# Copies that spread token lists move from GpSimd to DVE, and a slot loads all of the next w2 at its own end

## The chip, the cores and the metric

The kernel runs on one core of a Trainium2 chip. The metric is the device time of one execution in microseconds, as the median of several runs. The engines are named as the profile names them: PE (TensorE matmul) and PEld (its weight load), DVE (VectorE), ACT (ScalarE), POOL (GpSimd) and SP (SyncE, which here only issues transfers). A q behind an engine's name (SPq) means its instruction queue.

## The reference, cut to what matters

Attention with a sigmoid in place of the softmax is followed by a mixture of experts in which each token goes to one expert.

```python
def _attn_ref(q, k, v):                 # (8, 12, 448, 64) each
    scores = scale * q @ k.T - log(S)
    return (1 / (1 + exp(-scores))) @ v
...
def _moe_ref(x, w_gate, w_output_gate, w1, w2):   # x: (3584, 768), 8 experts
    logits = x @ w_gate
    e_idx = argmax(logits, axis=1)
    gate_w = softmax(logits)[e_idx]
    eom = sigmoid(x @ w_output_gate)
    for e in range(8):                  # w1[e]: (768, 1024), w2[e]: (1024, 768)
        mask = e_idx == e
        out[mask] = gate_w * eom[:, e] * (relu(x[mask] @ w1[e]) @ w2[e])
```

## The kernel before, in words

**Stages.** Up to about 270 us the kernel computes attention, batch after batch, writes the rows to DRAM (`x_dram`) and routes the finished batches: each token gets a place in its expert's list in DRAM (`lst`). After that it works through slots. A slot is one expert with up to 256 tokens of its list: layer 1 (x times w1, eight groups `f` of 128 hidden units), then layer 2 (h times w2, two halves of tokens by two halves of columns). PE computes in a split form: every operand is a high part, made by a cast on ACT, and a low part, made by a subtraction on DVE, so each weight that arrives is first split (`split_w1`, `split_w2`, lines 578 to 600).

**Kinds of slots.** In this execution there are eleven slots of 256 tokens (numbers 0 to 10, function `slot`), three of 192 tokens (`wide_slot`, 640 to 724 us) and two of 128 tokens (`half_slot`, from 724 us on). Slots 0 to 3 are straight code; the later ones stand in nested conditional blocks, since only the routing says how many of each kind there are. Where a block isn't entered, each engine jumps to the end of the nest and there raises the semaphores that the left-out code would have raised.

**The order of work in a slot.** The order on each engine is the order in which the program is written; nothing is reordered. In layer 1, group `f` of PE fills one of three PSUM banks (`self.psh`, cut to three at line 1048), ACT copies half of it (L631), DVE adds the other half (L632), ACT applies the ReLU (L636) and DVE makes the low part (L637). PE can't begin group f+3 before DVE's L632 of group f has read its bank. After layer 1 come, for the next slot: `turn_x` (a transposition of the gathered tokens on DVE, L605), the gather of the tokens of the slot after the next (POOL, indirect DMAs, L545, into the one buffer `xg` that `turn_x` has just read), the split of x and w1, and beside them PE's layer 2.

**Lists.** A gather needs its token numbers spread over 128 partitions, and so does the scatter of the output. `spread_lists` (L498), `spread_two` (L510) and `spread_rest` (L524) do that: DVE transposes a block of 32 partitions (L501, L513), and then POOL makes four times three small copies, one set of three for each group of 32 destination partitions, out of the same 32 source partitions. Two `spread_lists` of 12 copies stand in the attention stage (`unit`, u = -31 and -8). The rest is done from the generator `side()` (lines 1004 to 1045), which is advanced between the steps of slots 0 to 3: counting its steps, one `spread_lists` falls in slot 1 right behind `turn_x`, one `spread_two` in slot 2 behind group 2, one `spread_two` in the layer 2 of slot 2, and in slot 3 a `spread_lists` behind group 1, a `spread_lists` behind group 3 and `spread_rest` (8 small instructions) behind group 4. Slot 3 also has a POOL drain (L696) ahead of its gather.

**w2 around the 192-token slots.** w2 comes in four transfers of two rows of blocks each (rows 0, 2, 4, 6 of `w2r`). A 192-token slot uses raw w2 in `layer2_q` (L725) for 64 of its tokens, so `w2r` comes free late. It loads rows 0 and 2 of the next w2 behind `layer2_q` (L760), and at its end leaves the next expert's number and a flag in two words (`held`, DVE copy L764). The slot that follows, wide or half, begins with `load_held` (L574): SP loads two registers from those words (L539) and issues rows 4 and 6 (L566), then loads two registers for the slot after, and issues that slot's w1.

Of the kernel before, what the change touches and what calls it, by code (L numbers as in the profile page):

```python
# [42 lines left out]
LATE_F = LATE_MAX + 2  # L43
LATE_N = LATE_F + E + 2
GT = 32
LGR = LATE_N // 4
# [8 lines left out]
def r32(ap):  # L55
    return ap.bitcast(F32)


class Kernel:
# [80 lines left out]
    def constants(self):  # L140
        nc = self.nc
# [64 lines left out]
        own = gl[1].bitcast(I32)  # L206
        a = TS
# [10 lines left out]
        self.ltb = own[:, a:a + 2 * E].rearrange("p (k h w) -> p k h w", h=1, w=2)  # L218
        a += 2 * E
        self.at = own[0:GT, a:a + LGR + 1]  # L220
        a += LGR + 1
        self.held = own[0:1, a:a + 2]

    def row_words(self):
        v, tok = self.nc.vector, self.tok
# [181 lines left out]
    def table_late(self):  # L407
        v = self.nc.vector
# [9 lines left out]
        first = self.tmp_off  # L418
# [61 lines left out]
        v.tensor_copy(self.tab_l[:, 0], both(0)[0:1])  # L480
        v.tensor_copy(self.tab_b, T[0:1, :, 2, 0:E])
        v.tensor_copy(self.tot, end[0:1, :, E - 1])
        v.memset(self.held, 0)
        yield 1

    def take(self, key, tiles):
# [11 lines left out]
    def spread_lists(self, raw, lt, lx):  # L498
        nc, k, g = self.nc, lx.shape[1], lx.shape[2]
        t = self.take("lt32", self.lt32)  # L500
        nc.vector.transpose(t, raw.rearrange("p (t w) -> p w t", w=6))  # L501
        copy = nc.gpsimd.tensor_copy
        for i in range(4):
            r = slice(32 * i, 32 * i + 32)
            copy(lx[r], t[:, i, 0:k * g].rearrange("p (k g) -> p k g", g=g))
            own = t[:, :, 0:k * g].rearrange("p w (k h q) -> p w k h q", k=k, q=4)
            copy(lt[r, :, :, 0], own[:, 4, :, :, i])
            copy(r32(lt[r, :, :, 1]), own[:, 5, :, :, i])

    def spread_two(self, raw, lt, lx):  # L510
        nc, t = self.nc, self.lt32_two
        for j in range(2):
            nc.vector.transpose(t[:, j], raw[:, Q4 * j:Q4 * j + Q4].rearrange("p (t w) -> p w t", w=6))  # L513
        copy = nc.gpsimd.tensor_copy
        two = lambda a: a.rearrange("p (j k) g -> p j k g", j=2)
        for i in range(4):
            r = slice(32 * i, 32 * i + 32)
            copy(two(lx[r]), t[:, :, i].rearrange("p j (k g) -> p j k g", g=8))
            for w in range(2):
                to = lt[r, :, :, w]  # L520
                copy(two(r32(to) if w else to),
                     t[:, :, 4 + w].rearrange("p j (k h q) -> p j k h q", h=2, q=4)[:, :, :, :, i])

    def spread_rest(self):  # L524
        g = self.nc.gpsimd
        a = EARLY + LATE_F
        for i in range(4):
            r, q = slice(32 * i, 32 * i + 32), slice(32 * (i % 2), 32 * (i % 2) + 32)
            own = self.lts[q, a:, 1]
            g.tensor_scalar(self.ltq[r, :, 0], own[:, :, 0], 2.0, float(i // 2), ALU.mult, ALU.add)  # L530
            g.tensor_copy(r32(self.ltq[r, :, 1]), r32(own[:, :, 1]))
# [39 lines left out]
    def load_w2(self, s, rows=range(0, 8, 2)):  # L571
        if s is not None:
            self.load_w(s, self.w2, self.w2r, rows)

    def load_held(self):
        self.load_w2(self.slot_regs(self.held.unsqueeze(2), 0, 1), (4, 6))

    def split(self, raw, hi, lo):
        self.nc.scalar.copy(hi, raw)  # L579
# [152 lines left out]

    def wide_slot(self, j, hint):
        cur = self.wide_lists(j)
        if j:
            self.load_held()
        nx = self.load_slot(self.tab_l, LATE_F + j + 1, self.wide_lists(j + 1))
        self.nc.gpsimd.drain()
        self.split_w2(0)
        for f in range(8):  # L740
            if f == 6:
                self.finish()
            self.layer1(f, n=WS)
            if f == 0:
                hint()
            if f:
                self.high_low(f - 1, HS)
            if f in (1, 3, 5):
                self.split_w2(f // 2 + 1)
        self.high_low(7, HS)  # L750
        self.high_w1(0)
        self.turn_x(nx)
        self.gather(self.wide_lists(j + 2))
        for k in range(3):
            self.split_x(nx, k)
        self.low_w1(0)
        self.split_w1(1)
        self.split_w1(2)
        self.layer2_q(cur, self.ys[0])
        self.load_w2(nx, (0, 2))  # L760
        self.layer2(cur, 0, 0, self.ys[1], self.psy[1])
        self.layer2_due(cur, 0)
        k = LATE_F + j + 1
        self.nc.vector.tensor_copy(self.held, self.tab_l[0:1, 0:3:2, k])  # L764

    def half_slot(self, j, y):
        nc = self.nc
        nx = None
        if j == 0:
            self.load_held()  # L770
        if j + 1 < E:
            nx = self.load_slot(self.tab_b, j + 1, self.half_lists(j + 1))
        if j:
            if nx is not None:
                self.gather(self.half_lists(j + 1))
            nc.gpsimd.drain()  # L776
        (wh, wl), (xh, xl), (hh, hl) = self.w1s, self.xs, self.hs

        def turn(n):
            ps = self.take("x", self.psx).rearrange("p a (b t) -> p (a b) t", b=2)  # L780
            for i in range(4):
                nc.tensor.transpose(ps[:, i], self.hb[:, 128 * (4 * n + i):128 * (4 * n + i + 1)], self.ident)  # L782
            fs = slice(4 * n, 4 * n + 4)
            self.split(ps, hh[:, fs, 0:HS], hl[:, fs, 0:HS])

        w2 = [self.w2_rows(k) for k in range(4)]
        low = lambda k: nc.vector.tensor_tensor(w2[k][2], w2[k][0], r32(w2[k][1]), ALU.subtract)
        for n in range(2):
            c = slice(512 * n, 512 * n + 512)
            ps = self.take("h", self.psh)  # L790
            for d in range(6):
                if n == 1 and d == 3:
                    turn(0)
                    low(2)
                    nc.scalar.copy(w2[3][1], w2[3][0])  # L795
                    low(3)
                nc.tensor.matmul(ps, xh[:, d, 0:HS], wh[d][:, c], start=(d == 0), stop=False)
                nc.tensor.matmul(ps, xh[:, d, 0:HS], wl[d][:, c], start=False, stop=False)
                nc.tensor.matmul(ps, xl[:, d, 0:HS], wh[d][:, c], start=False, stop=(d == 5))
            if n == 0:  # L800
                self.split_w2(0)
                self.split_w2(1)
            nc.scalar.activation(self.hb[:, c], ps, AF.Relu)  # L803
            if n == 0:
                nc.scalar.copy(w2[2][1], w2[2][0])
        cur = dict(lt=self.ltb[:, j])
        pss = self.psy[0:2]
        self.layer2_mm(pss[0], 0, 0, range(2))
        turn(1)
        if j == 0:  # L810
            self.finish()
        if nx is not None:
            self.turn_x(nx)
            self.split_w1(0)
            for k in range(3):
                self.split_x(nx, k)
            self.split_w1(1)
        self.layer2_mm(pss[0], 0, 0, range(2, 4))
        self.layer2_mm(pss[1], 0, 1, range(4))
        self.load_w2(nx)  # L820
        if nx is not None:
            self.split_w1_row(4)
        for n in range(2):
            self.layer2_mm(pss[n], 0, n, range(4, 8))
            self.layer2_out(pss[n], cur, 0, n, y)
        if nx is not None:
            self.split_w1_row(5)
# [296 lines left out]
```

## Time and profile before

| what | value |
|---|---|
| median of 3 runs | 770.81 us (770.23 to 771.84) |
| profiled execution, its own time | 771.06 us |
| its span in the trace | 769.2 us |
| granted TensorE clock over the span | 0.997 of full speed |

The span is the time between the first and the last instruction in the trace; the 1.9 us around it belong to the execution too. The profiled execution is 0.25 us above the median.

### The profile page before, as it was taken

To read this page: it belongs to the slowest core of one execution; us is meant where nothing else is said; L and a number is where in the kernel's file an instruction comes from. 1 tells how busy PE (TensorE), PEld (TensorE's weight loads), DVE (VectorE), ACT (ScalarE), POOL (GpSimd) and SP (SyncE) were. 2 spreads that over 40 slices of the span, in tenths; PEclk is the share of its full clock that TensorE was granted. 3 is DMA by queue.
4 is the path that set the end of the run, shared out by engine and by line. 5 is a ranking of instruction groups with operands and counts; after the bars stand their busy time and mean duration, and the time that the engine had idled before them with its cause. 6 is when DMAs were issued, how large, how long until landed. Compare 5 with 4: busy or idle time off the path is not lost. (4 is left out here: it accounts for less than half of the span.)

```text
span 769.2 us, 15280 instructions
## 1 busy us (share of the span) xinstructions
PE 756.5 (98%) x5823; PEld 581.5 (76%) x5823; DVE 493.9 (64%) x846; ACT 488.4 (63%) x654; POOL 338.0 (44%) x393
## 2 busy tenths in 40 slices
PE   9999999999999999999999999999999999999996
PEld 4457754444434389899998989999899999889785
DVE  3333345435476679967786676858577685887787
ACT  5666656666687756566665565756556574675685
POOL 5000003232154555787885647355372633633522
PEclk9999999999999999999999999999999999999998
DMA  7464544536486340256766497511156755497691
GB/s 257 145 216 138 203 164 146 159 131 217 145 319 246 122 162 1 80 202 221 260 229 225 170 322 287 157 52 41 42 218 212 268 159 215 145 351 255 224 397 47
DMA packets 43790, 145.21 MB, mean 189 GB/s; under 512 B 5671, under 2 KB 7951, under 8 KB 42672
## 3 DMA queue, kind: packets, MB, share of 16 engines
q1 hardware_dynamic: 33872, 119.56, 43.9%
q0 software_dynamic: 9824, 24.46, 9.4%
q8 instruction: 50, 0.82, 0.4%
q14 instruction: 44, 0.36, 0.1%
HBM read 152.61 MB, written 23.06 MB: 228 GB/s over the span
## 5 line engine op out<-in xcount | busy, mean ns | idle before, releaser
L623 PE MATMUL ps<-rounded 128*128 128x512 f32 (+1 forms) x672 | 226.2, 386 | 1.1 <-PEq L1066 0.8
L871 ACT ACTIVATE a<-ps,bias_s 128x896 f32<-128x896 f32 x168 | 169.0, 1008 | 87.1 <-PE ps L869 87.0
L545 POOL DMA_INDIRECT plain<-x_dram,lxs x122 | 180.4, 1479 | 67.9 <-issue 32.2
L869 PE MATMUL ps<-kqv 64*64 64x448 f32 x1344 | 194.3, 542 | 0.0
L878 PE MATMUL ps<-a,kqv 64*64 64x448 f32 x1344 | 192.4, 536 | 0.0
L624 PE MATMUL ps<-rounded 128*128 128x256 f32 (+1 forms) x672 | 184.1, 274 | 1.2 <-DVE due L658 1.2
L648 PE MATMUL ps<-w2h,h 128*128 128x384 f32 x432 | 145.0, 336 | 0.0
L580 DVE TENSOR_TENSOR w2l<-plain,w2h 128x1536 fp32r<-128x1536 f32 x60 | 105.3, 1757 | 61.9 <-ACT w2h L579 61.9
L650 PE MATMUL ps<-w2h,h 128*128 128x384 f32 x432 | 144.5, 334 | 0.0
L649 PE MATMUL ps<-w2l,h 128*128 128x384 f32 x432 | 144.5, 334 | 0.0
L623 PEld LDWEIGHTS ps<-rounded 128*128 128x128 f32 x672 | 125.9, 187 | 24.3 <-issue 2.0
L624 PEld LDWEIGHTS ps<-rounded 128*128 128x128 f32 x672 | 127.3, 189 | 1.6 <-DVE rounded L586 1.6
L869 PEld LDWEIGHTS ps<-kqv 64*64 64x64 f32 x1344 | 66.3, 134 | 67.2 <-issue 52.9
L878 PEld LDWEIGHTS ps<-a,kqv 64*64 64x64 f32 x1344 | 67.5, 133 | 60.8 <-issue 51.9
L586 DVE TENSOR_TENSOR rounded<-plain,rounded 128x2048 fp32r<-128x2048 f32 x46 | 103.4, 2286 | 2.6 <-ACT rounded L583 2.6
L631 ACT COPY gl<-ps 128x256 f32<-128x256 f32 (+1 forms) x112 | 40.4, 361 | 95.3 <-PE ps L624 89.4
L579 ACT CAST w2h<-plain 128x1536 fp32r<-128x1536 f32 x60 | 88.0, 1470 | 16.6 <-PE ps L914 4.8
L583 ACT CAST rounded<-plain 128x2048 fp32r<-128x2048 f32 x46 | 87.2, 1902 | 0.0
L648 PEld LDWEIGHTS ps<-w2h,h 128*128 128x128 f32 x432 | 81.1, 188 | 2.4 <-issue 1.8
L649 PEld LDWEIGHTS ps<-w2l,h 128*128 128x128 f32 x432 | 81.2, 188 | 0.1
L650 PEld LDWEIGHTS ps<-w2h,h 128*128 128x128 f32 x432 | 81.1, 188 | 0.0
L670 POOL DMA_INDIRECT out<-y,due x11 | 18.2, 1651 | 114.2 <-ACT gl L631 92.8
(257 smaller groups left out, 685.0 us busy)
## 6 DMA issues: line engine op xcount, KB each, us to landing
plain<-w SPq DMA_DIRECT2D x68, 768.0 KB
plain<-w SPq DMA_DIRECT2D x48, 1024.0 KB
kqv<-kqv SPq DMA_DIRECT2D x23, 1344.0 KB
x_dram<-xt SPq DMA_DIRECT2D x8, 1344.0 KB
plain<-w SPq DMA_DIRECT2D x6, 512.0 KB
plain<-x_dram,lxs POOLq DMA_INDIRECT x122, 4.3
kqv<-kqv SPq DMA_DIRECT2D x2, 448.0 KB
lst<-plain POOLq DMA_DIRECT2D x1, 726.0 KB, 6.8
```

The lines of the kernel that those rows point to most:

```text
L545: self.nc.gpsimd.indirect_dma_start(out=s["xg"][:, g], out_offset=None, in_=x4, in_offset=bass.IndirectOffsetOnAxis(ap=s["lx"][:, g:g + 1] ...
L579: self.nc.scalar.copy(hi, raw)
L580: self.nc.vector.tensor_tensor(lo, raw, r32(hi), ALU.subtract)
L586: self.nc.vector.tensor_tensor(self.w1p[1][k], self.w1r[:, 2 * k:2 * k + 2], r32(self.w1p[0][k]), ALU.subtract)
L623: nc.tensor.matmul(out, wh[d][:, c], both, start=(d == 0), stop=False)
L624: nc.tensor.matmul(ps[:, 0:n], wl[d][:, c], self.xc[:, d, 0, 0:n], start=False, stop=(d == 5))
L648: nc.tensor.matmul(ps, hh[:, f, tk], wh, start=(f == 0), stop=False)
L649: nc.tensor.matmul(ps, hh[:, f, tk], wl, start=False, stop=False)
L650: nc.tensor.matmul(ps, hl[:, f, tk], wh, start=False, stop=(f == 7))
L869: nc.tensor.matmul(ps[half[h], j, 0:S], kg[half[j], e, 1, o:o + 64], kg[half[j], e, 0], start=True, stop=True)
L871: nc.scalar.activation(at[u % 4], ps[:, :, 0:S], AF.Sigmoid, bias=self.bias_s, scale=1.0 / math.sqrt(D))
L878: nc.tensor.matmul(self.ps_o[e][h][half[j], 0:S], v[half[h], 6 if i == 3 else 3 * e + c, j], a[half[h], j], start=(i in ((0, 3 if h else 4 ...
```

## The change

The copies of the three spreading functions are issued to DVE in place of POOL; nothing else in them changes. The words `held`, the DVE copy that fills them and `load_held` are gone. A 192-token slot now loads rows 4 and 6 of the next w2 itself at its end, each behind a DVE copy of one element of that row onto itself; the transfer overwrites that element and so waits for the copy. The registers are those that the slot has already loaded for rows 0 and 2 (`nx`).

```diff
     def spread_lists(self, raw, lt, lx):
-        copy = nc.gpsimd.tensor_copy
+        copy = nc.vector.tensor_copy
...
     def spread_two(self, raw, lt, lx):
-        copy = nc.gpsimd.tensor_copy
+        copy = nc.vector.tensor_copy
...
     def spread_rest(self):
-        g = self.nc.gpsimd
+        g = self.nc.vector
...
-    def load_held(self):
-        self.load_w2(self.slot_regs(self.held.unsqueeze(2), 0, 1), (4, 6))
...
     def wide_slot(self, j, hint):
         cur = self.wide_lists(j)
-        if j:
-            self.load_held()
...
         self.load_w2(nx, (0, 2))
         self.layer2(cur, 0, 0, self.ys[1], self.psy[1])
         self.layer2_due(cur, 0)
-        k = LATE_F + j + 1
-        self.nc.vector.tensor_copy(self.held, self.tab_l[0:1, 0:3:2, k])
+        for q in (4, 6):
+            first = self.w2r[0:1, q, 0:1]
+            self.nc.vector.tensor_copy(first, first)
+            self.load_w2(nx, (q,))
 
     def half_slot(self, j, y):
         nx = None
-        if j == 0:
-            self.load_held()
```

The memory of `held` (two words behind `self.at`) and its clearing in `table_late` (L483) go too.

## Rows read from the trace of the kernel before

**Rows 1.** The page's first part: busy time and share of each engine.
```profile
PE 756.5 (98%) x5823; PEld 581.5 (76%) x5823; DVE 493.9 (64%) x846; ACT 488.4 (63%) x654; POOL 338.0 (44%) x393
```
**Rows 2.** Waits of PE, whole span: us in total, times, longest.
```profile
PE ps L624 <- DVE due L658: 1.2, 1, 1.2
...
PE ps L782 <- ACT hb L803: 1.2, 1, 1.2
...
PE ps L623 <- DVE gl L632: 0.3, 1, 0.3
```
**Rows 3.** Timeline of DVE in slot 4: start, us, what, idle before.
```profile
431.35 1.78 DVE L605 STREAM_TRANSPOSE plain<-plain 128x1536 f32<-128x1536 f32 x1 [6.77 <-DMA plain<-x_dram,lxs]
```
**Rows 4.** Timeline of POOL from slot 3's last spreads on.
```profile
393.39 0.20 POOL L505 CAST lxs<-wg 32x32 int32<-32x32 f32 x1
...
416.55 1.04 POOL L545 DMA_INDIRECT plain<-x_dram,lxs  x1 [8.03 <-DVE h L637]
```
**Rows 5.** Timeline of DVE in the attention stage, behind an early spread.
```profile
260.96 0.62 DVE L885 COPY xh<-ps 128x448 f32<-128x448 f32 x1 [1.73 <-PE ps L878]
```
**Rows 6.** Timeline of DVE in slot 1: two small casts in a row.
```profile
319.76 0.16 DVE L480 CAST gl<-hb 1x24 int32<-1x24 f32 x1
319.84 0.16 DVE L481 CAST gl<-hb 1x24 int32<-1x24 f32 x1
```
**Rows 7.** Timeline of POOL: copies of one spread, across a change of destination partitions.
```profile
339.57 0.20 POOL L507 CAST lts<-lt 32x8 int32<-32x8 f32 x1
339.71 0.19 POOL L508 COPY lts<-lt 32x8 f32<-32x8 f32 x1
339.95 0.20 POOL L505 CAST lxs<-lt 32x32 int32<-32x32 f32 x1
```
**Rows 8.** Timeline of DVE in slots 2 and 3.
```profile
360.61 1.78 DVE L605 STREAM_TRANSPOSE plain<-plain 128x1536 f32<-128x1536 f32 x1 [2.67 <-DMA plain<-x_dram,lxs]
...
372.93 0.97 DVE L513 STREAM_TRANSPOSE lt_two<-hb 32x192 f32<-32x192 f32 x2 [1.24 <-POOL lts L521]
...
381.74 0.37 DVE L632 TENSOR_TENSOR gl<-gl,ps 128x256 f32<-128x256 f32 x1
...
386.11 0.37 DVE L632 TENSOR_TENSOR gl<-gl,ps 128x256 f32<-128x256 f32 x1
...
391.94 1.78 DVE L605 STREAM_TRANSPOSE plain<-plain 128x1536 f32<-128x1536 f32 x1
```
**Rows 9.** Timeline of PE in slot 3: first matmul of layer 1's last group.
```profile
387.24 0.39 PE L623 MATMUL ps<-rounded 128*128 128x512 f32 x1
```
**Rows 10.** The chain that ended last, at the first half slot: start, us, what.
```profile
723.72 0.28 SPq L539
...
725.61 0.40 SPq L566
...
726.64 7.71 DMA plain<-w
```
**Rows 11.** Timeline of ACT in the first half slot.
```profile
730.50 1.48 ACT L805 CAST w2h<-plain 128x1536 fp32r<-128x1536 f32 x1 [0.20 <-DMA plain<-w]
...
734.43 1.48 ACT L795 CAST w2h<-plain 128x1536 fp32r<-128x1536 f32 x1 [1.61 <-DMA plain<-w]
...
738.16 1.91 ACT L583 CAST rounded<-plain 128x2048 fp32r<-128x2048 f32 x1
```
**Rows 12.** SP at the end of the wide blocks: xcount, duration ns, first and last start.
```profile
L1071 SPq EVENT_SEMAPHORE  x9: 17/17/17, 718.8 to 721.0; - x9
L1071 SPq COMPARE_BRANCH  x2: 43/46/50, 714.0 to 721.0; - x2
```
**Rows 13.** SP's transfers of the next w1 and w2, first half slot.
```profile
729.22 4.13 SPq L566 DMA_DIRECT2D plain<-w  x5
```
**Rows 14.** One stretch: PE, PEld, DVE, ACT, POOL busy, PE clock, DMA share, GB/s.
```profile
730.00:732.00 2.00, 2.00 (x13) 1.68 (x12) 0.00 (x0) 1.78 (x2) 0.00 (x0) 1.00 1.02 410
```
**Rows 15.** Waits of PE's weight load, whole span.
```profile
PEld ps L798 <- DVE rounded L580: 0.3, 1, 0.3
```

More of the change, by code (lines that the diff above doesn't have):

```diff
@@ L220, in constants @@
         self.at = own[0:GT, a:a + LGR + 1]
-        a += LGR + 1
-        self.held = own[0:1, a:a + 2]
     def row_words(self):
@@ L482, in table_late @@
         v.tensor_copy(self.tot, end[0:1, :, E - 1])
-        v.memset(self.held, 0)
         yield 1
```

## The prediction

> **What bounds the kernel now.** The page's first part is read first: PE is busy for 98% of the span and no other engine for more than 64% [rows 1]. So a change pays only where PE stands still, and costs only where it makes PE stand still. The waits of PE are the second view, and they are few. The two that this change can reach are one wait of 1.2 us behind DVE's L658 and one of 1.2 us behind ACT's L803; a third, of 0.3 us, is for DVE's L632 and shows the rule of the three PSUM banks at work: when DVE is late with its addition, PE can't open the group three further on [rows 2]. The third view is the timeline, to see what stands behind each.
>
> The first wait is at the border of slots 4 and 5. L658 is a tiny copy that stands on DVE behind the split of w1, and that stands behind turn_x, which idled 6.77 us for gathered tokens, until 431.35 [rows 3]. The gather was late because POOL was: its 32 instructions for the lists began at 393.39, POOL was idle for the last 8.03 us before 416.55 (a drain), so they had taken 15 us, and the first gather came at 416.55 [rows 4], though the buffer it fills had been free since slot 3's turn_x ended at 393.72 [rows 8].
>
> The second is in the first half slot. The chain of work goes from SP's register load at 723.72 over two transfers, at 725.61 and 726.64, to the landing at 734.35 [rows 10]; ACT's cast of w2's last rows idled 1.61 us for it [rows 11], and L803, queued behind that cast, kept PE's transpositions waiting.
>
> **The change, part by part.**
>
> *What the copies cost on DVE.* The trace has no such copy on DVE, so it is bounded. Below: two small casts that don't depend on each other start 0.08 us apart though each lasts 0.16 [rows 6]; twelve copies, a third of them with 32 or 64 elements, make 1.0 us. Above: each waits for the end of the one before, 0.17 apart, 2.1 us. Between: POOL's own copies overlap inside a set (0.14 apart at 0.20 long) and not where the destination changes to the next 32 partitions (0.24 apart) [rows 7]. The same pattern on DVE is 0.08 + 0.08 + 0.17 per set, 1.3 for four, with the longer elements 1.4 us. I take 1.4, since these are the same copies in the same order. [...]
>
> *The two early spreads.* Behind the second DVE idles 1.73 us for PE before its next copy [rows 5], so 1.4 us disappear there. The first pushes DVE's work on attention by up to 1.4 us; PE has no wait of note for DVE in that stage [rows 2], whose sums have half a group of units in hand. Counted at nothing; without that cover 1.4 each.
>
> *Slot 1.* Twelve copies behind turn_x move the w1 split by 1.4. Its last part is needed only when PE is four blocks into the next slot; the same place in slot 4 was 1.2 us too late only after a delay of 6.77 [rows 2, 3]. Nothing. POOL in turn no longer makes 2 us of copies ahead of its gather, so the 2.67 us that turn_x of slot 2 idles shrink by about 2 [rows 8].
>
> *Slot 2.* Twelve copies behind group 2 have DVE finish group 4's addition 1.4 later. In slot 3, below, that addition has 0.76 us in hand after a start made late by 1.24 us of waiting for POOL [rows 8], which slot 2 doesn't have: about 2.0 in hand, so nothing is counted (at 0.76 it would be 0.65). In its layer 2 twelve copies come in, and those 1.24 us go out; with the earlier turn_x DVE enters slot 3 about 0.5 us sooner.
>
> *Slot 3.* This is where it costs. Twelve copies land ahead of group 2's addition (381.74) and twelve more ahead of group 4's (386.11) [rows 8]. In between DVE and ACT hand each other work in turn (addition, ReLU, cast of w2, its low part), so the first delay is not made up before the second comes. Group 4's addition ended at 386.48 and PE opened the last group at 387.24 [rows 9]: 0.76 in hand. Then 386.48 - 0.5 + 2 x 1.4 = 388.8: PE waits 1.55 us. With copies at 1.0 it is 0.75, with 2.1 it is 2.95. The eight instructions of the rest come behind that addition and delay only low parts that layer 2 takes last.
>
> *Slot 4.* POOL is rid of the 15 us, the drain starts when its last scatter is out, and the gather can start when slot 3's turn_x is through, about 396 even with DVE 2 us late. At the pace of before (416.55 to the end of the idle time at 431.35 [rows 3, 4]), 14.8 us, the tokens are there at 411, before turn_x is due at 425. The wait of 1.2 us goes: -1.2.
>
> *w2 at the end of the wide slot.* The one-element copies stand on DVE where the copy L764 stood, one small instruction more per wide slot (0.08 [rows 6]), with nothing due on DVE for that time. SP waits for them to the same moment, about 723.7, but needs no registers and has no block to enter: transfers at 723.8 and 724.7 in place of 725.61 and 726.64 [rows 10]. The first landed at about 730.45, 4.85 after its issue [rows 10, 11]; at 410 GB/s [rows 14] a transfer of 768 KB takes 1.9. So they land at 728.7 and 730.6, ACT's cast of the last rows needn't idle from 732.82 to 734.43 [rows 11], and PE's 1.2 us go. In the first two borders, wide to wide, no PE wait stands, so the same 1.9 us bring nothing.
>
> But SP now has these transfers ahead of its jump. Before, it branched at 714.0, came to the end of the nest at 718.8 and was through its nine semaphore instructions at 721.0, all in time that it had [rows 12]. Nine instructions of 17 ns don't fill those 2.2 us; what was still in flight then was rows 0 and 2 of w2, and I read them as a wait for its landing. After, the branch is at 725.1, the end of the nest at 729.9, and the semaphores wait for the landing at 730.6, until 731.0. Two branches, registers and issue, 1.9 us as from 723.72 to 725.61 [rows 10], and 0.3 bring the first transfer of the half slot's w1 to 733.2, where it was at 729.22 [rows 13]. It lands 4.85 + 0.6 (the larger size) later, 738.7 at most. ACT's L583, which starts on it, stood at 738.16 [rows 11], and would want to start 1.2 us earlier. From there on DVE is without a gap until the last split of w1, for which PE's load already waits by 0.3 [rows 15]. So the 1.2 us won are lost again in the second half slot, and 0 to 0.5 more: +0.3. The bounds: -1.2 if the semaphores don't wait for landings; +2.5 if the second transfer lands 3.9 behind the first, as it did before (730.45 to 734.35), and w1 then comes 2 us later still.
>
> **Sum.** +1.55 (slot 3) - 1.2 (slot 4) + 0.3 (half slots) = +0.65 us on the profiled execution's 771.06, 771.7; the median lies 0.25 below that execution, so 771.5.
>
> **Rivals.** *Slower:* the copies on DVE don't overlap at all. Slot 3's wait is then 2.95 in place of 1.55, and the sum +2.05: 772.9. It decides from 1.85 us per spread on, 0.155 per copy (PE wait 2.45, sum +1.55). For it: they go to four groups of partitions and POOL's copies don't overlap across those; against it: DVE's casts do overlap when nothing stands between them [rows 6, 7]. *Slower too:* w1 late by the upper bound, sum +2.85: 773.7. For it: w2's second transfer did take 3.9; against it: w1's transfers were then sharing the queues, which they now can't. *Faster:* SP's jump isn't held by landings, so the half slots keep their 1.2 us, and DVE's copies are at the lower bound: 0.75 - 1.2 - 1.2 = -1.65, 769.2. For it: before, the branch came so early that the trace can't tell what its semaphores wait for; against it: the 2.2 us of rows 12. *The gather stays late,* because the drain takes its 8 us wherever it starts: it would then end near 404 and the tokens come at 419, still in time; so this changes nothing unless the drain waits for something in slot 4, which gives +1.85, 772.7.
>
> **How the numbers follow.** A measurement of this kernel tells about 0.2%, 1.5 us, from no change. The forecast, within that, has 0.51; within it fall all mixtures of the middle values. Slower has 0.30: copies without overlap 0.15, w1 later 0.10, gather still late 0.05. Faster has 0.19: the jump unhindered with cheap copies, or cheap copies with slot 3 covered by more of an early start than 0.5. The range goes from the faster rival, 769.2, to between the two slower ones, 773.4. The likeliest case alone has 769.9 to 772.3.
>
> **What would show it.** In the profile after: in slot 3 a wait of PE's L623 for DVE's L632 of 1 to 2 us, and sets of twelve small DVE copies lasting 1.0 to 2.1 us; no POOL copies behind 393, a gather of slot 5's tokens that begins near 396 and no wait of PE at 440; SP's two transfers at the end of the third wide slot 1.9 us earlier against the rest of it, then a gap in SP of 6 us and in the DMA queues of some 2 us; no wait of PE for L803 in the first half slot, and a new one for DVE's L580 or L586 in the second. It would be wrong if PE in slot 3 runs through (then -1 us), if SP goes on without the gap (-1.2), or if a stage that has no wait now, the attention stage above all, gets one from DVE.

## The result and the profile after

The changed kernel takes 780.21 us (median of 4 runs, 778.74 to 782.16) beside 770.52 us for the kernel before (768.2 to 771.84): ratio 1.0131, 95% interval 1.0094 to 1.0167. It is slower by some 10 us; the forecast was 771.5, and the range ended at 773.4. The profiled execution took 779.01 us with a span of 777.2, 8.0 more than before.

The first part of the page and PE's waits, after (L617 is the L623 of before, L774 the L782, L626 the L632, L789 the L797; L795 is ACT's ReLU of the half slot, before L803):

```profile
PE 757.8 (98%) x5823; PEld 584.0 (75%) x5823; DVE 504.3 (65%) x940; ACT 488.3 (63%) x654; POOL 301.8 (39%) x301
```

```profile
PE ps L774 <- ACT hb L795: 6.9, 1, 6.9
PE ps L617 <- DVE gl L626: 2.2, 3, 1.3
```

The busy times have hardly moved [rows 1]; the waits have [rows 2]. Slot 3 has a wait for DVE of 1.9 us more in all, the wait of 1.2 us at the border of slots 4 and 5 is gone, and the wait of 1.2 us in the first half slot has become one of 6.9 us. The timelines of ACT and PE there, after:

```profile
735.81 2.84 ACT L573 CAST w2h<-plain 128x1536 fp32r<-128x1536 f32 x2 [14.24 <-SPq L1063]
738.56 0.59 ACT L795 ACTIVATE hb<-ps 128x512 f32<-128x512 f32 x1
```

```profile
731.88 0.39 PE L791 MATMUL ps<-rounded 128*128 128x512 f32 x1
739.20 1.11 PE L774 MATMUL ps<-ident,hb 128*128 128x128 f32 x4 [6.94 <-ACT hb L795]
...
740.54 0.63 PE L790 MATMUL ps<-rounded 128*128 128x512 f32 x1
...
742.95 0.39 PE L790 MATMUL ps<-rounded 128*128 128x512 f32 x1
```

ACT's first two casts of w2 wait 14.2 us, not for data (rows 0 and 2 go out behind `layer2_q`, some 11 us before the slot's end, as in the kernel before, and by the trace's landing records they are there by 720.5) but for SP's instruction queue at L1063, the end of the wide nest. The ReLU that PE wants stands behind these casts. And PE, after standing idle, works slower: a matmul of 0.39 us takes 0.63. Windows of the changed kernel (PE, PEld, DVE, ACT, POOL busy, PE clock, DMA share, GB/s):

```profile
736.00:738.00 2.00, 0.00 (x0) 0.00 (x0) 0.69 (x1) 2.00 (x2) 0.00 (x0) 0.50 0.00 0
740.00:742.00 2.00, 2.00 (x7) 1.61 (x6) 1.71 (x3) 2.00 (x3) 0.00 (x0) 0.50 1.00 412
```

The granted clock went to 0.50 while PE stood, and its next block is short of about 1.7 us: from the first transposition to the eighth matmul behind the four it takes 3.75 us (739.20 to 742.95), where the kernel before, at a granted clock of 1.00, takes 2.05 (731.55 to 733.60):

```profile
731.55 0.60 PE L782 MATMUL ps<-ident,hb 128*128 128x128 f32 x4
...
733.60 0.39 PE L798 MATMUL ps<-rounded 128*128 128x512 f32 x1
```

The account of the span: +5.7 (half slot's wait), +1.7 (clock), +1.9 (slot 3), -1.2 (slot 4) is +8.1, against 8.0.

What SP does, after: its two transfers, and the instructions of the nest's end (xcount, duration ns, first and last start).

```profile
724.56 1.22 SPq L563 DMA_DIRECT2D plain<-w  x2
```

```profile
L1063 SPq EVENT_SEMAPHORE  x9: 17/17/17, 731.5 to 735.7; - x9
...
L1063 SPq COMPARE_BRANCH  x2: 43/46/50, 725.8 to 735.7; - x2
```

SP leaves at 725.8, executes the first instruction of the nest's end at 731.5, 5.7 us later, and needs 4.2 us for nine instructions of 17 ns. The way from the branch to the first instruction at its target, 5.7 us here, is called the jump below. Before, the same stretch ran from 714.0 to 721.0 [rows 12], while PE was still in the wide slot.

### The profile page after: what moved, and what is told of

It reads as the page before. It is cut to its first block, busy times and chain, and to the rows that moved or that the text cites. A ratio compares the mean times of both kernels' runs of the same rounds, so it can differ in the third digit from the quotient of the medians.

```text
span 777.2 us, 15272 instructions
## 1 busy us (share of the span) xinstructions
PE 757.8 (98%) x5823; PEld 584.0 (75%) x5823; DVE 504.3 (65%) x940; ACT 488.3 (63%) x654; POOL 301.8 (39%) x301
## 5 line engine op out<-in xcount | busy, mean ns | idle before, releaser
L617 PE MATMUL ps<-rounded 128*128 128x512 f32 (+1 forms) x672 | 226.5, 387 | 3.0 <-DVE gl L626 2.2
L542 POOL DMA_INDIRECT plain<-x_dram,lxs x122 | 182.7, 1498 | 86.8 <-DVE plain L599 51.2
L861 PE MATMUL ps<-kqv 64*64 64x448 f32 x1344 | 176.5, 540 | 0.0
L870 PE MATMUL ps<-a,kqv 64*64 64x448 f32 x1344 | 175.1, 536 | 0.3 <-DMA kqv<-kqv 0.3
L617 PEld LDWEIGHTS ps<-rounded 128*128 128x128 f32 x672 | 125.8, 187 | 26.6 <-DVE gl L626 3.3
L573 ACT CAST w2h<-plain 128x1536 fp32r<-128x1536 f32 x60 | 87.9, 1469 | 27.5 <-SPq L1063 14.2
L664 POOL DMA_INDIRECT out<-y,due x11 | 20.0, 1815 | 134.4 <-ACT gl L625 115.5
```

Source lines behind the costliest of these rows:

```text
L542: self.nc.gpsimd.indirect_dma_start(out=s["xg"][:, g], out_offset=None, in_=x4, in_offset=bass.IndirectOffsetOnAxis(ap=s["lx"][:, g:g + 1] ...
L617: nc.tensor.matmul(out, wh[d][:, c], both, start=(d == 0), stop=False)
L861: nc.tensor.matmul(ps[half[h], j, 0:S], kg[half[j], e, 1, o:o + 64], kg[half[j], e, 0], start=True, stop=True)
L870: nc.tensor.matmul(self.ps_o[e][h][half[j], 0:S], v[half[h], 6 if i == 3 else 3 * e + c, j], a[half[h], j], start=(i in ((0, 3 if h else 4 ...
```

## The experiments

Intervals are those of the ratio to the kernel before on the same chip; its medians were 769.22 (beside `copies_only`, `w2_only`, `w2_early` and `tiny_end`), 770.13 (`dummy_two`, `dummy_one`, `copies_hop` and `held_one_late`) and 769.09 (`one_at_end`, `held_one`, `late_held` and `late_pool`).

**The two parts alone.** `copies_only` is the kernel before with `copy = nc.vector.tensor_copy` in the three spreading functions; `w2_only` is the changed kernel with `nc.gpsimd` there.

> The kernel before, with only the copies moved to DVE (held words and load_held stay). Queue theory (the time is lost at the end of the wide slots, because SP goes to the end of the nest behind the two transfers and only then raises the semaphores that the first half slot's ACT and DVE wait for): the two PE waits of slot 3 come (+2.2 us), the one of slot 4 goes (-1.4 us), the half slots stay as before: +0.8 us, 771.3. Rival, copies (DVE as a whole is too late): most of the 9.7 us are here, 777 or more.

> The changed kernel with the copies back on POOL. Queue theory: slots 3 and 4 as before, in the first half slot the same PE wait of about 7.1 us (1.35 before) and 1.4 us of matmuls at the lower clock behind it: +7.1 us, 777.6. Rival, copies: within 1 us of 770.5.

Measured: `copies_only` 771.44 us, ratio 1.0016 (1.0000 to 1.0032); `w2_only` 777.35, ratio 1.0100 (1.0079 to 1.0121). PE's waits in the one and in the other:

```profile
PE ps L623 <- DVE gl L632: 2.2, 3, 1.4
PE ps L782 <- ACT hb L803: 1.4, 1, 1.4
```

```profile
PE ps L774 <- ACT hb L795: 6.9, 1, 6.9
```

The loss is w2's part. The copies cost about a microsecond, 1.9 us more in slot 3 less the 1.2 of slot 4 by the profiles; by the times alone that is hardly told from none, and the 1.2 isn't there in every execution (see slot 4 below).

**When the transfers go out.** `w2_early` loads all four parts behind `layer2_q` and has nothing at the slot's end; `tiny_end` adds a transfer of 8 bytes at the end, behind a DVE copy. Both keep the copies on POOL.

```diff
-        self.load_w2(nx, (0, 2))
+        self.load_w2(nx)
 ...
-        for q in (4, 6):
-            ...
+        self.nc.vector.tensor_copy(self.word, self.word)                    # tiny_end only
+        self.nc.sync.dma_start(self.word, self.w2[bass.ds(nx["e"], 1), 0, 0:2], cond=nx["chg"] > 0)
```

> The kernel before, POOL copies kept; a 192-token slot loads all four parts of the next w2 right behind layer2_q, with nothing behind DVE at its end. Queue theory: SP's branch comes 1.7 us later than before, the end of the nest and the landings are reached before 727, ACT's first cast of the half slot is not late, and the last cast of w2 has its data: the 1.2 us wait of before goes too, 769.3. Rival, late data (the casts wait for w2's own landing, whichever way SP goes): the same, since the data land early; a rival that blames DMA traffic with four transfers in a row: 772 or more.

> As the kernel with all of w2 behind layer2_q, and at the slot's end one DVE copy of two words onto themselves and a transfer of 8 bytes over them, whose data nobody reads. All of w2 is there by 726. Queue theory: SP branches at about 724.8, reaches the end of the nest at 730.5, and the landing of 8 bytes is over by then; ACT's first cast of the half slot starts at about 730.8 in place of 735.8 in the changed kernel and 724.8 in the kernel before, PE waits about 2.1 us for ACT's relu (7.1 less 5.0), the clock does not fall: 2 to 3.5 us over the kernel without the tiny transfer. Rival, late data: no wait, the same time as without it.

Measured: 770.77 us, ratio 1.0012 (0.9996 to 1.0029), and 770.47, ratio 1.0005 (0.9990 to 1.0020). Both expectations missed. SP and ACT at the nest's end in `w2_early`, then its longest wait of PE; and SP, PE's longest wait and ACT's ReLU in `tiny_end`:

```profile
L1059 SPq EVENT_SEMAPHORE  x9: 17/17/17, 720.7 to 725.9; - x9
L1059 SPq COMPARE_BRANCH  x2: 43/46/50, 715.4 to 726.0; - x2
...
L1059 ACTq COMPARE_BRANCH  x2: 38/44/50, 719.4 to 725.8; - x2
...
L1059 ACTq EVENT_SEMAPHORE  x1: 17/17/17, 725.7 to 725.7; - x1
```

```profile
PE ps L785 <- ACTq L1059: 2.3, 1, 2.3
```

```profile
L1064 SPq EVENT_SEMAPHORE  x9: 17/17/17, 727.1 to 727.7; - x9
...
L1064 SPq COMPARE_BRANCH  x2: 43/46/50, 723.8 to 727.8; - x2
```

```profile
PE ps L790 <- ACTq L1064: 2.2, 1, 2.2
```

```profile
731.18 0.60 ACT L796 ACTIVATE hb<-ps 128x512 f32<-128x512 f32 x1 [0.47 <-PE ps L792]
```

In `w2_early` the wait for the last cast is gone, but ACT's jump takes 6.3 us (719.4 to 725.7) with four transfers on their way, and PE waits 2.3 us for ACT's semaphore instead, where before it waited 0.7 us at this entry: nearly an equal exchange. In `tiny_end` SP too leaves only at the slot's end, as in the changed kernel, but little is then in flight (0.30 MB from 723.8 to 727.2): the jump takes 3.3 us, not 5.7, the nine instructions 0.6 us, not 4.2, and there is no wait for the ReLU. That doesn't show that a late jump alone is free: PE enters this half slot 2.2 us late, by the same exchange, and the ReLU has 0.5 us in hand. Had PE waited only 0.7 us at the entry, it would have stood for about 1 us at the ReLU (an estimate, 2.2 less 0.7 and 0.5).

**Transfers that nobody reads.** `dummy_two` and `dummy_one` are `tiny_end` with two or one transfers of 768 KB to a scratch buffer in DRAM behind the tiny one.

```diff
+        for q, junk in zip((4, 6), self.junk):      # dummy_one has one buffer, q = 4
+            self.nc.sync.dma_start(junk.unsqueeze(0),
+                self.w2[bass.ds(nx["e"], 1), 128 * q:128 * q + 256], cond=nx["chg"] > 0)
```

> tiny_end with two transfers of 768 KB behind the tiny one at the slot's end, from rows 4 and 6 of the next w2 to a scratch buffer in DRAM that nobody reads. All of the w2 that the half slot uses has landed by 726, as in tiny_end. Queue theory: SP's jump is among the packets of the transfers again (5 to 6 us in place of the 3.3 of tiny_end), then SP waits for the second landing, ACT's first cast of the half slot starts at about 735 though its data are nearly 10 us old, PE waits about 7 us for the relu, and the clock falls behind it: 7 to 9 us over tiny_end, 777 to 779. Rival, late data (what counts is when the w2 that is read lands): no wait of PE there, the time of tiny_end within 1 us.

> As dummy_two with one transfer of 768 KB in place of two. Queue theory: the wait is as long as the last landing is late. One transfer lands 4.8 to 6.6 us after its issue, at 729 to 731, so SP is through its semaphores at about 731 and ACT's first cast starts there: PE waits 2 to 3 us, the clock stays: 2 to 3 us over tiny_end. Rival, jump alone (the loss is SP's slow jump, the landings don't matter): the same jump as with two, so the same loss as dummy_two within 1 us.

Measured: `dummy_two` 776.48 us, ratio 1.0081 (1.0056 to 1.0106); `dummy_one` 770.12, ratio 1.0004 (0.9990 to 1.0019). SP, then ACT's first cast and PE's wait, in `dummy_two`; and SP in `dummy_one`:

```profile
L1067 SPq EVENT_SEMAPHORE  x9: 17/17/17, 731.1 to 733.0; - x9
...
L1067 SPq COMPARE_BRANCH  x2: 38/44/50, 723.7 to 733.0; - x2
```

```profile
733.11 2.85 ACT L577 CAST w2h<-plain 128x1536 fp32r<-128x1536 f32 x2 [14.06 <-SPq L1067]
```

```profile
PE ps L778 <- ACT hb L799: 5.2, 1, 5.2
```

```profile
L1067 SPq EVENT_SEMAPHORE  x9: 17/17/17, 727.6 to 728.2; - x9
...
L1067 SPq COMPARE_BRANCH  x2: 38/44/50, 722.8 to 728.3; - x2
```

With data that nobody reads most of the loss comes back, though all of the w2 that the half slot reads has landed by 723.9: late data as the cause is out. (The profiled execution of `dummy_two` is the slowest of its four, 780.32 us.) Its 9.3 us from SP's branch to the last of the nine are divided otherwise than in the changed kernel: 7.4 are the jump, 1.4 a wait and 0.5 the instructions. With one transfer SP is through at 728.3, where about 731 was expected, and the 2 to 3 us did not come: PE had entered this half slot 2.2 us late (the exchange of `w2_early`) and at a granted clock of 0.51 (726 to 728 us), and that covered it. The rival, the same loss as `dummy_two`, did not come either; its jump was shorter too, 4.8 us. So this run says little about how late ACT may be; the next says more.

**One real transfer at the end.** `one_at_end` is the changed kernel with row 4 moved to the early loads: `self.load_w2(nx, (0, 2, 4))`, and `for q in (6,)` at the end.

> The changed kernel with one transfer in place of two at the end of a 192-token slot: rows 0, 2 and 4 of the next w2 behind layer2_q, row 6 behind its one-element copy; copies on DVE as changed. From dummy_one: SP is through its semaphores at about 728.5, ACT's first cast starts at 728.5 to 729.5, which is about as late as it may. PE waits 0 to 1 us for the relu in place of 6.9, the clock stays, the 1.35 us of before are gone, slot 3 keeps its 2.2: within 1 us of before, 8 to 10 us under the changed kernel. Rival, late data (row 6 is issued at the same late moment as before and lands no sooner): the half slot waits for row 6 as long as the changed kernel did, 5 us or more.

Measured: 773.86 us, ratio 1.0048 (1.0025 to 1.0071), which is between the two theories' figures. Its longest wait of PE, and SP:

```profile
PE ps L774 <- ACT hb L795: 2.7, 1, 2.7
```

```profile
L1063 SPq EVENT_SEMAPHORE  x9: 17/17/17, 730.3 to 730.9; - x9
...
L1063 SPq COMPARE_BRANCH  x2: 43/46/50, 724.6 to 731.0; - x2
```

The jump takes 5.7 us again, among the packets of one transfer (0.79 MB from 724.6 to 730.4); the nine instructions then run in 0.6 us, for it has landed meanwhile. This splits the changed kernel's 9.9 us from 725.8 to 735.7: 5.7 are the jump, 3.6 the wait for the second landing, 0.6 the instructions. ACT started at 731.09 here and PE waited 2.7, so 728.4 was the latest start without a wait, 3.0 behind PE's entry at 725.4. The clock, which was expected to stay, fell here too (0.59 granted from 736 to 738 us): the block that takes 2.05 us at a clock of 1.00 took 3.55 (734.49 to 738.04).

That SP waits for landings can be read from the trace's landing records. In the changed kernel the last part of the second transfer lands at 735.13, and the second of the nine instructions starts at 735.15; in the kernel before a landing at 720.87 is followed by an instruction at 720.89. In each of the nine profiles in which SP is held among the nine instructions, it goes on within 0.02 us of a landing.

**The order of the copies.** `copies_hop` is `copies_only` with the loops of `spread_lists` exchanged, so that every copy goes to another group of 32 partitions than the one before.

> copies_only with the twelve copies of spread_lists in another order: the same word for all four groups of partitions, then the next word, so that each copy goes to another group of 32 partitions than the one before. If DVE holds a copy when the destination group changes (0.17 apart) and not within a group (0.08 apart, as in the trace after), a spread takes 2.0 us in place of 1.45, and the two that stand in front of slot 3's additions make PE's wait there 1.1 us longer, 3.3 in place of 2.2: 1.1 us over copies_only. If the order doesn't matter: the time of copies_only.

Measured: 774.22 us, ratio 1.0069 (1.0043 to 1.0095). PE's waits for this addition come to 3.8 us, 1.6 more than in `copies_only`, and the span to 772.2, 1.7 more. DVE in slot 3, `copies_hop`:

```profile
380.89 0.73 DVE L506 CAST lxs<-wg 32x32 int32<-32x32 f32 x4
381.63 0.69 DVE L508 CAST lts<-wg 32x8 int32<-32x8 f32 x4
382.33 0.69 DVE L510 COPY lts<-wg 32x8 f32<-32x8 f32 x4
383.06 0.42 DVE L634 TENSOR_TENSOR gl<-gl,ps 128x256 f32<-128x256 f32 x1
```

The twelve take 2.17 us (380.89 to 383.06) in place of 1.45: they start 0.18 apart in the mean at 0.16 to 0.17 long, each behind the end of the one before. By the ratios the two differ by 0.53%, 4.1 us, which is more than the 1.7 of the profiles; the medians lie 4.1 and 2.2 us over those of the kernel before, 1.9 apart. The two were timed on different chips, and two of the seven runs of `copies_hop` took over 777 us, which the medians leave out; why they did isn't explained.

**A faster version.** `held_one_late`, with the copies on DVE, keeps the held words for row 6 alone and moves slot 3's last spreads; `held_one` does only the first on the kernel before, `late_held` only the second (with the copies on DVE), `late_pool` the second with the copies on POOL.

```diff
-        self.load_w2(self.slot_regs(self.held.unsqueeze(2), 0, 1), (4, 6))
+        self.load_w2(self.slot_regs(self.held.unsqueeze(2), 0, 1), (6,))
 ...
-        self.load_w2(nx, (0, 2))
+        self.load_w2(nx, (0, 2, 4))
 ... in side():
+            for _ in range(8):
+                yield
             self.spread_lists(self.lr[5], *at(20, 4))
-            yield
-            yield
             self.spread_lists(self.lr[6], self.ltb, self.lxb)
-            yield
             self.spread_rest()
```

> An attempt at a faster version: the kernel before with the copies on DVE, but slot 3's two spreads and the rest moved to the end of its layer 2 (nothing there needs them before slot 7), and rows 0, 2 and 4 of the next w2 behind layer2_q, only row 6 behind the held words. Expected: no wait of PE in slot 3 (-2.2 against copies_only), no wait at the border of slots 4 and 5 (-1.2 to -1.4 against before), and the last cast of w2 in the first half slot no longer late (-1.2), if the three transfers are through before ACT and DVE jump to the end of the nest at 718.6 to 720.5: 2.6 us under before, 767. If the third transfer is still in flight then, their jumps take 6 us in place of 3, and PE enters the half slot 1.5 us later: 768.5.

> The kernel before with its POOL copies in their place; rows 0, 2 and 4 of the next w2 behind layer2_q and only row 6 by the held words. Expected from the profile of held_one_late: the 1.2 us of slot 4 stay, the 1.2 to 1.4 us of the first half slot go, nothing comes at its entry: 1.3 us under before, ratio 0.998. If the third transfer slows the jumps of ACT and DVE by more than they have in hand: no gain.

> held_one_late with the w2 loads of the kernel before (rows 0 and 2 early, 4 and 6 by the held words): the copies on DVE, slot 3's two spreads and the rest at its end. Order theory (the copies cost only where they stand ahead of an addition that frees a PSUM bank): no wait in slot 3, none at the border of slots 4 and 5, the 1.2 to 1.4 us of the first half slot stay: 1.3 us under before, ratio 0.998. Rival, copies cost DVE time wherever they stand: within 0.5 us of copies_only, 1 us over before.

> The kernel before, copies on POOL, with only the order changed: slot 3's two spreads and the rest at its end, behind the gather. Order theory: the gather for slot 5 starts near 396, the wait at the border of slots 4 and 5 goes though no copy has left POOL, 1.2 to 1.4 us under before. Rival, engine theory (POOL is too slow for these copies wherever they stand): 15 us of copies hold up the scatters and drain of slot 4, and a wait of 1 us or more comes there.

Measured: `held_one_late` 767.36 us, ratio 0.9976 (0.9962 to 0.9990); `held_one` 768.40, 0.9974 (0.9953 to 0.9995); `late_held` 768.84, 0.9984 (0.9964 to 1.0005); `late_pool` 768.87, 0.9988 (0.9965 to 1.0012). All waits of PE in `held_one_late`:

```profile
PE ps L923 <- DVE rounded L919: 1.2, 1, 1.2
PE ps L797 <- ACTq L1070: 0.8, 1, 0.8
PE ps L623 <- PEq L1065: 0.7, 1, 0.7
PE ps L623 <- DVE gl L632: 0.3, 1, 0.3
```

None is left in slots 3 and 4 or within the half slots, and it beats both kernels. In `late_pool` no copy has left POOL, but the gather no longer stands behind the copies, and slot 4's `turn_x`, which idled 6.77 us before [rows 3], doesn't idle (POOL and DVE, `late_pool`):

```profile
399.65 1.16 POOL L545 DMA_INDIRECT plain<-x_dram,lxs  x1 [9.94 <-issue]
```

```profile
424.15 1.77 DVE L605 STREAM_TRANSPOSE plain<-plain 128x1536 f32<-128x1536 f32 x1
```

The profiles show both mechanisms; of the two orders alone the times can't tell a gain from none. Of `held_one` the interval can, though narrowly: its median is only 0.7 us under that of the kernel before.

## Why the prediction was wrong

**The step that failed** is "w2 at the end of the wide slot", costed at +0.3 us, upper bound +2.5; it cost 7.4 (5.7 and 1.7), and alone, in `w2_only`, 7.7 (1.0% of 770). It asked what SP's semaphores at the nest's end hold up, and answered: SP's next transfers. It did not ask who else waits for them. ACT's and DVE's split of rows 0 and 2 in the half slot waits for the counts that SP raises there, though the data have long landed, so SP's delay went onto PE's path in the middle of the first half slot, 6.9 us and the clock behind it, not only onto w1 for the second. `dummy_two` shows it: PE waits 5.2 us there with all of the data early. No rival of the prediction had this place.

**Its durations were short as well.** The jump was taken at 4.8 us, from the branch before, and took 5.7. The landing of the second transfer was forecast at 730.6 with a bound of 3.9 us behind the first; it came at 735.1, 4.0 behind the first and 3.6 behind the jump's end. So the -1.2 of this part had no ground either: counted from PE's entry into the half slot, row 6 was issued 1.8 us earlier than before and still landed 0.2 us later (9.2 against 9.0). That the nest's end waits for landings was read rightly from the 2.2 us of [rows 12]: nine instructions take 0.6 us when nothing is in flight and up to 5.2 when four transfers are. The rival "the jump unhindered" is out.

**What the 1.2 us of before were.** The prediction expected them to go and be lost again in the second half slot. That slot has no new wait; `held_one` shows that they go for good when row 4 is early.

**Slot 3: right, mis-sized by 0.3.** A spread took 1.45 us (1.4 forecast), and the wait rose by 1.9 (1.55 forecast, bounds 0.75 to 2.95), 0.5 of it already behind the first spread and 1.3 behind the second. DVE, after:

```profile
381.72 0.17 DVE L502 CAST lxs<-wg 32x32 int32<-32x32 f32 x1
381.81 0.15 DVE L504 CAST lts<-wg 32x8 int32<-32x8 f32 x1
381.89 0.15 DVE L505 COPY lts<-wg 32x8 f32<-32x8 f32 x1
382.06 0.17 DVE L502 CAST lxs<-wg 32x32 int32<-32x32 f32 x1
...
388.60 0.42 DVE L626 TENSOR_TENSOR gl<-gl,ps 128x256 f32<-128x256 f32 x1
```

Copies start 0.08 apart within a group of destination partitions and 0.17 apart where it changes (once 0.26 in slot 3). In `copies_hop`, where it changes from each copy to the next, all start 0.18 apart in the mean. That DVE would follow the pattern of POOL's copies [rows 7] was the author's estimate, and these two traces bear it out. The addition of group 4 ended at 389.02, forecast 388.8.

**Slot 4 and the rest: the mechanism right, its size less sure.** The gather begins at 396.63 (forecast about 396), there is no wait at the border, and neither the early spreads nor slots 1 and 2 gave PE a wait.

```profile
396.63 0.98 POOL L542 DMA_INDIRECT plain<-x_dram,lxs  x1 [14.95 <-DVE plain L599]
```

`late_pool` adds that moving the copies behind the gather ends the idle time of `turn_x` as well as moving them to DVE. But PE's 1.2 us, taken from one profile, aren't in every execution with the copies on POOL in their old place. Of seven such profiles three (`w2_only`, `dummy_one` and `dummy_two`) have no wait of PE at this border, with `turn_x` idle for 3.6 to 4.6 us; the four others have one, with 6.8 to 7.4. In `w2_only`:

```profile
427.85 1.78 DVE L599 STREAM_TRANSPOSE plain<-plain 128x1536 f32<-128x1536 f32 x1 [3.83 <-DMA plain<-x_dram,lxs]
```

**The clock** stood in no term of the sum: 1.7 us, lost at a granted clock of 0.50 behind the idle time of 6.9 us.

## What to carry to other kernels

Where an engine jumps over blocks that aren't entered, count with everything behind its arrival: the jump (3.3 to 7.4 us of SP in these runs), the landings of its own transfers (3.6 us more in the changed kernel), and every engine that waits for a count it raises, even for data long there (14.2 us of ACT). Issue large transfers either so early that they have landed before the engines jump (ACT's jump took 2.6 to 3.3 us with two early loads, 6.2 to 6.4 with four), or behind the jump; where neither fits all of them, split them, as three early and one behind did here. Work that an engine must do between two steps of a chain costs by its place: the same copies on DVE cost 1.9 us ahead of two additions, and at the slot's end they left PE no wait, on either engine.

## What the runs showed of the hardware

**The jump took less time when little was in flight.** From the branch to the first instruction at the nest's end, in us:

| engine | little in flight | 768 KB transfers on their way |
|---|---|---|
| SP | 3.3 (`tiny_end`) | 4.8 to 6.2 with one to four (4.8 before, 5.7 after), in no order of their number; 7.4 in `dummy_two` |
| ACT | 2.6 (after) to 3.3 (`copies_only`) with two early loads, landed or nearly | 3.6 to 4.5 with three early loads (`held_one`, `one_at_end`, `held_one_late`); 6.2 to 6.4 with four (`w2_early`, `tiny_end`, `dummy_one`, `dummy_two`) |

The page's DMA part, for the 5.8 us of SP's jump after (packets, MB, share of 16 engines), shows two packets of the kind instruction among the data:

```profile
q1 hardware_dynamic: 492, 1.44, 73.8%
...
q8 instruction: 1, 0.02, 1.0%
q14 instruction: 1, 0.01, 0.3%
```

In 3.4 us of `tiny_end` that hold its jump (723.8 to 727.2) there are three such packets. That these packets are the code at the jump's target, and that it waits behind the data, is the author's estimate from the table; the traces don't show it. The transfers of `dummy_two` go from DRAM to DRAM.

**The clock after an idle time isn't the same each time.** PE stood 2.2 us at the entry of the half slot in `dummy_one` and worked on at 0.51 of full clock; in `dummy_two` it stood 2.3 us at the same place and the clock stayed at 1.00. In `w2_early` and `tiny_end` it stood 2.3 and 2.2 us there, and the clock over the whole span was 0.998 and 0.999 (0.996 in `dummy_one`). Behind the 2.7 us of `one_at_end` it fell, to 0.59 from 736 to 738 us. The same window of `dummy_one` and of `dummy_two`:

```profile
726.00:728.00 2.00, 2.00 (x6) 1.52 (x6) 0.00 (x0) 0.00 (x0) 0.00 (x0) 0.51 0.48 145
```

```profile
726.00:728.00 2.00, 2.00 (x11) 1.65 (x10) 0.00 (x0) 0.00 (x0) 0.00 (x0) 1.00 1.33 336
```
